# Load order, load sizes and due times in a fused sliding-window attention and squared-ReLU feed-forward kernel

## The chip, the cores and the metric

The kernel runs on one core of one Trainium2 chip. The metric is the device time of one execution in microseconds (us); before the change its median over five runs is 309.8 us (309.5 to 310.71). A core has five engines that run side by side: TensorE (PE) for matrix products and transposes, with its weight loads (PEld), VectorE (DVE), ScalarE (ACT), GpSimd (POOL) and SyncE (SP). In this kernel POOL and SP mostly issue transfers between the chip's memory and the core's own; sixteen DMA engines carry them out.

## The reference

```python
# q, k, v: 8 batches, 8 heads, 576 positions, 64 channels, float32
scores = scale * np.matmul(q, k.transpose(0, 1, 3, 2))      # scale = 1/8
bias = slopes[:, None, None] * (-np.abs(rel))[None]         # rel = query pos - key pos
mask = (rel >= 0) & (rel < 128)
scores = np.where(mask, scores + bias[None], -1e9)
attn = softmax(scores)
x = np.matmul(attn, v)               # then (8*576, 512): heads side by side
h = x @ w_in                         # w_in: 512 x 2048
g = np.maximum(h, 0.0) ** 2
out = g @ w_out                      # w_out: 2048 x 512, out: 4608 x 512 float32
```

A query sees itself and the 127 positions before it, so a block of 128 queries needs the keys of its own block and of the block before.

## The kernel before

Each batch of 576 positions is cut into five blocks, four of 128 and one of 64, so there are 40 blocks, b0 to b39. The 4608 tokens are also cut into nine groups of 512 for the feed-forward part, whose hidden width of 2048 is cut into 16 slices of 128 (the code calls one slice `fc`).

**One block of attention.** POOL loads k, q and v of a block from float32 to bf16 (line 445); SP loads k and q of block 0 alone as float32 (437). k and q are transposed so that channels lie on the partitions: block 0 on TensorE in float32 (497), blocks 1 to 8 on TensorE in bf16 (515), with copies out by DVE or ACT (462, 464), and blocks 9 to 39 by a DMA transpose that SP issues (487). This makes a tile `kqT`. The score products of one or more blocks then run as one uninterrupted run of small matmuls on quarters or halves of the array (`burst`, 570 and 579). ACT takes exp: into tiles `raw` for the blocks that are cut into quarters (612), into `P` for the others (645). DVE multiplies by a mask that holds window and bias (627, 652). TensorE multiplies P by v, with a column of ones that yields the row sum (673). DVE divides (696, 701) and leaves a tile `x`. `x` is turned into `xT` by TensorE for the blocks listed in `X_PE` (719) and by a DMA transpose from SP for the others (711).

**Feed-forward.** `fc_step` (777) multiplies 4 chunks of `w_in` with a stretch of `xT` into a bank of 512 columns: one slice for 512 tokens, two for 256, four for 128. `SPLIT` says into which token ranges groups 0 and 1 are cut; all others are taken whole. ACT applies ReLU (786), DVE squares (793). `t_part` (840) multiplies by `w_out`, sixteen matmuls into one bank for each 128 tokens; ACT copies out (809) and a DMA stores (817), nearly always from SP.

**What sets the order.** All work is first entered in a list of tasks, each with a key. `Plan.order` walks through an assumed time: on each engine it takes the task that can start first and, among equals, the one with the smallest key, and writes the order down. The emitted program keeps this order on every engine; each engine runs its own list in order and stops where an operand is not there. Keys of the loads at the start follow the string `FIRST`, in which `b3` is block 3 (its k, q and v), `i0` the first piece of `w_in` and `o0` the first quarter of `w_out`; `V0` makes v of block 0 a little later. `W_IN` gives the limits of the pieces of `w_in` in slices. Keys of the attention of a block follow from the token at which it is due, less `AHEAD` for that block (or `LEAD`); `EARLY` shifts the first-layer work of group 1. `KQ_PE` and `X_PE` list the blocks that TensorE transposes. Score runs join the halves of several blocks: two halves to a run below block `LONG`, and `UNITS` from it on. `MARGIN` is a time that the planner adds to each landing of a transfer. `SHARE` and `SOON` limit how many banks the feed-forward part may take when a score run is near. At most eight transfers of POOL are under way: the next one waits for the landing of the one eight before.

**Filler.** While the planner expects TensorE to have nothing to do, matmuls on a tile of zeros are put in (`idle`, 880): `WARM` units of 128 columns at the very start, later a share `FILL` of each expected gap up to `UNTIL`. `COLD` is the time up to which the planner counts TensorE's work double.

Of the kernel before, what the change touches and what calls it, by code (L numbers as in the profile page):

```python
# [243 lines left out]
def kernel(  # L244
# [15 lines left out]
    NG = NT // 512  # L260
    NBLK = B * NKB

    FIRST = "b0 b1 b2 b3 i0 i1 o0 b4 i2 b5 i3 o1 b6 b7 o2 b8 o3 b9"
    SPLIT = {0: [(0, 256), (256, 512)], 1: [(0, 192), (192, 320), (320, 512)]}
    EARLY = -60
    AHEAD = {10: -60, 1: 0, 4: 90, 9: 90, 5: -30, 0: -60, 12: 60, 11: 0, 2: 90, 8: 90, 7: 0, 6: 0, 3: -30, 24: 30, 14: 60, 18: 30, 25: 90, 23: 0, 16: 60, 13: 90, 21: 0, 19: -60, 17: 0, 22: 0, 20: 0, 15: 30}
    LEAD = 0

    KQ_PE = [0, 1, 2, 3, 4, 5, 6, 7, 8]
    X_PE = [0, 1, 2, 3, 4, 5, 6, 7, 8, 10, 12]  # L270
    WARM = 20
    FILL, UNTIL = 0.9, 26e3
    COLD = 12000
    QUARTERS = 6
    V0 = 2
    SHARE, SOON = 3, 1000
    MARGIN = 500
    LONG, UNITS = 5, 3
    W_IN = [0, 4, 8, 12, 16]
    PAIR_AFTER, PAIR_KEY = 1, -100  # L280
    BANKS = {"A": 8}
    HOLD, OSB = 12, 14
# [17 lines left out]
    def ring(name, n, shape):  # L300
        return [const.tile(shape, BF16, name=f"{name}_{i}") for i in range(n)]


    size = {"kq": 6, "v": 6, "kqT": 5, "P": 2, "x": 4, "Pq": 2, "raw": 2}
    kq = ring("kq", size["kq"], [128, 2, d_model])
    vt = ring("vt", size["v"], [128, H, D + 1])
    kqT = ring("kqT", size["kqT"], [128, 2 * C, 128])
    Pt = {nm: ring(nm, size[nm], [128, H, 2, 128]) for nm in ("P", "Pq")}
    raw = ring("raw", size["raw"], [128, H, 256])
    xt = ring("x", size["x"], [128, d_model])  # L310

    plan = Plan({"rec": 4, "rt": 3, "g": 2, "osb": OSB, **size}, BANKS, COLD, (SHARE, SOON))
    banks = {tag: [psum.tile([128, 512], FP32, name=f"{tag}_{i}", bufs=1) for i in range(n)] for tag, n in BANKS.items()}
# [84 lines left out]
    def warm():  # L398
        idle(bank(sw), WARM)
    sw = Slot("A")  # L400
    tw = plan.add({"PE": 53.5 * WARM}, -9.1e5, warm, [t_ones], [sw], [sw])
    tw.cols, tw.n = 128 * WARM, -(-WARM // 4)

    def load(key, ns, emit, deps=(), acq=(), cost=13.6):
        return plan.add({"POOL": 900.0}, key, emit, deps, acq, dma=("w", ns, cost))
# [4 lines left out]
    def load_w_in(n, key):  # L410
        lo, hi = 128 * W_IN[n], 128 * W_IN[n + 1]

        def emit():
            nc.gpsimd.dma_start(w_in_sb[:, :, lo:hi], moe_w_in[:, lo:hi].rearrange("(c p) f -> p c f", p=128))  # L414
        t = load(key, {256: 1400.0, 512: 2600.0}[hi - lo] + (700.0 if n == 0 else 0.0), emit, cost=80.0)
        t_win[W_IN[n]:W_IN[n + 1]] = [t] * (W_IN[n + 1] - W_IN[n])

# [32 lines left out]

    for i, what in enumerate(FIRST.split()):
        {"b": load_block, "i": load_w_in, "o": load_w_out}[what[0]](int(what[1:]), -9e5 + i)
# [13 lines left out]
    def where(m):  # L466
        b, kb = divmod(m, NKB)
        return b, kb, blk[kb], (b * S + kb * 128 + blk[kb]) / 4 - 192 - 40 - AHEAD.get(m, LEAD if m not in X_PE else 0), b == 0

    def bank(slot):  # L470
        if slot.tile is None:
            slot.tile = banks[slot.tag][slot.idx]
            if slot.turns:
                slot.tile = slot.tile.bitcast(BF16)
        return slot.tile
# [181 lines left out]
    def mix(m):  # L657
        b, kb, n, due, first = where(m)
        x_by_dma = m not in X_PE
        parts = parts_of[m]  # L660
# [101 lines left out]
    def fc_step(g, unit, key, lo=0, hi=512):  # L762
        if g not in g_slots:
            g_slots[g] = Slot("g")
            g_sq[g] = [[] for _ in range(FCB)]
        sg = g_slots[g]
        w = hi - lo
        per = 512 // w
        slot = Slot("A")
        slot.ffn = True  # L770
        fcs = range(unit * per, min(FCB, (unit + 1) * per))
        cols = len(fcs) * w
        last = None
        for fi, fc in enumerate(fcs):
            for cc in range(C):
                def emit(cc=cc, fc=fc, fi=fi):
                    nc.tensor.matmul(bank(slot)[:, fi * w:(fi + 1) * w], w_in_sb[:, cc, fc * 128:(fc + 1) * 128],  # L777
                                     xT[:, cc, g * 512 + lo:g * 512 + hi], start=cc == 0, stop=cc == C - 1)
                last = plan.add({"PE": mm(w)}, key + (fi * C + cc) * w / 512, emit,
                                [last, t_win[fc]] + tokens(g * 512 + lo, g * 512 + hi),  # L780
                                [slot, sg] if cc == 0 and fi == 0 else [])
        srt = Slot("rt")

        def relu():
            srt.tile = work.tile([128, 512], BF16, tag="rt", bufs=3, name="rt")
            nc.scalar.activation(srt.tile[:, 0:cols], slot.tile[:, 0:cols], AF.Relu, bias=0.0, scale=1.0)  # L786
        tr = plan.add({"ACT": act(cols)}, key, relu, [last], [srt], [slot])

        def square():
            if sg.tile is None:  # L790
                sg.tile = work.tile([128, FCB, 512], BF16, tag="g", bufs=2, name="g")
            r = srt.tile[:, 0:cols].rearrange("p (f w) -> p f w", f=len(fcs))
            nc.vector.tensor_tensor(sg.tile[:, fcs[0]:fcs[-1] + 1, lo:hi], r, r, op=ALU.mult)  # L793
        ts = plan.add({"DVE": dve(cols, 2)}, key, square, [tr], [], [srt])
        for fc in fcs:
            g_sq[g][fc].append((lo, hi, ts))
# [3 lines left out]
    LAST = [(0, 384), (384, 512)]  # L800
    odd = (2 + NBLK - len(KQ_PE) + NBLK - len(X_PE) + NG * 4 + 1) % 8

# [57 lines left out]
    def steps(g):  # L860
        return [(u, lo, hi) for lo, hi in SPLIT.get(g, [(0, 512)]) for u in range(-(-FCB // (512 // (hi - lo))))]

# [4 lines left out]
    for g in range(NG):  # L867
        todo = steps(g + 1) if g + 1 < NG else []
        each = 64 / max(1, len(todo))
        for u in range(16):  # L870
            for x in todo[u * len(todo) // 16:(u + 1) * len(todo) // 16]:
                fc_step(g + 1, x[0], key + (EARLY if g == 0 else 0), *x[1:])
                key += each
# [3 lines left out]
    def idle(tile_, n):  # L877
        for i in range(0, n, 4):
            w = min(4, n - i)
            nc.tensor.matmul(tile_[:, 0:128 * w].rearrange("p (w x) -> p w x", w=w), zero,  # L880
                             zero.unsqueeze(1).to_broadcast([128, w, 128]), start=True, stop=True)

    def filler(slot, n):
        def emit():
            bank(slot)
            idle(banks[slot.tag][slot.idx], n)
        t = Task({"PE": 53.5 * n}, 0, emit, [t_ones], [slot])
        t.eng, t.start, t.end, t.seq, t.cols, t.n = "PE", 0.0, 0.0, 0, 128 * n, -(-n // 4)
        return t

    def fill(tasks):
        at, out = 0.0, []
        for t in tasks:
            if t.eng == "PE":
                slots = [s for s in t.acq if s.tag in BANKS]
                if slots and at and t.start < UNTIL:
                    n = int((t.start - at) * FILL / (107.0 if t.start < COLD else 54.0))
                    if n > 0:
                        out.append(filler(slots[0], n))
                at = t.start + t.engs["PE"] * (2 if t.start < COLD else 1)  # L900
            out.append(t)
        return out

    done = fill(plan.order(MARGIN))
    with tc.manual_schedule():
# [32 lines left out]
```

## Time and profile before

| What | Value |
| --- | --- |
| Median of five runs | 309.8 us |
| The profiled execution | 309.5 us, its span 307.7 us |
| Granted TensorE clock | 1.00 |
| PE busy | 301.0 us, 98% |
| DVE, ACT, POOL busy | 170.8, 170.5, 107.4 us |
| DMA queue of POOL (q0) | 114896 packets, 18.88 MB |
| DMA queue of SP (q1) | 53696 packets, 20.65 MB |
| L840, second layer | 592 matmuls, 146.3 us |
| L777, first layer | 768 matmuls, 145.3 us |
| L880, filler | 30 matmuls |
| L719, x turns on TensorE | 44 matmuls (11 blocks) |

Matmuls overlap, so the duration of one (373 ns on average at L840) is longer than the distance from one start to the next; the timeline's stretches show that distance (20 matmuls of 512 columns in 4.32 us on the chain, 216 ns each). "A <- B" names the tile written and the tiles read; the name after an arrow in brackets is what ended the wait before the instruction. A line number is that of the listing above.

### The profile page before, as it was taken

Reading aid. Unit: us, or ns where it says so; the run is one execution under the profiler, and the core shown is the slowest. Engines: PE = TensorE matmul, PEld = TensorE weight load, DVE = VectorE, ACT = ScalarE, POOL = GpSimd, SP = SyncE. Lnnn points to the kernel's source line nnn. Section 1 sums busy time; section 2 is a strip of 40 time slices with the busy share of each in tenths; the row PEclk is TensorE's granted clock in tenths of the full one; section 3 lists DMA queues with packets and bytes.
Section 4 is the critical chain, followed back from the end, with each engine's and each line's share of the span. In section 5 each row is a group of like instructions: output and inputs, shape, how many; then the busy total and the mean of one; then the engine's idle time right before and its main releaser. Section 6 shows DMA issues by size and latency. Waiting matters only on the chain.

```text
span 307.7 us, 7879 instructions
## 1 busy us (share of the span) xinstructions
PE 301.0 (98%) x3138; PEld 168.0 (55%) x3138; DVE 170.8 (55%) x563; ACT 170.5 (55%) x338; POOL 107.4 (35%) x134
## 2 busy tenths in 40 slices
PE   7799999999999999999999999999999999999996
PEld 3478877785555455455544454455445454444443
DVE  7774767757368865666754674376457552222200
ACT  4965775485157854664664673367366544344411
POOL 8937578545556446055333352110100000000100
PEclk9999999999999999999999999999999999999999
DMA  9999999999999999999999999579911111000022
GB/s 130 151 190 187 175 185 146 143 151 149 127 147 177 134 162 177 118 124 123 156 219 218 164 170 151 134 135 187 208 53 53 52 52 46 34 34 36 34 99 72
DMA packets 168629, 40.04 MB, mean 130 GB/s; under 512 B 159952, under 2 KB 164304, under 8 KB 168592
## 3 DMA queue, kind: packets, MB, share of 16 engines
q0 software_dynamic: 114896, 18.88, 85.3%
q1 hardware_dynamic: 53696, 20.65, 37.7%
q8 instruction: 24, 0.39, 0.5%
q14 instruction: 13, 0.11, 0.1%
HBM read 36.70 MB, written 9.44 MB: 150 GB/s over the span
## 4 chain that ended last, share of the span: by engine, by line
PE 92%; POOL 3%; DMA 3%; issue 0%; DVE 0%; POOLq 0%
PE A L840 41%; PE A L777 40%; PE A L673 5%; DMA w_in_sb<-in_moe_w_in_dram 3%; PE A L570 3%; POOL kq L445 2%; PE A L579 1%; POOL vt L445 1%; PE A L515 1%; PE A L719 1%; POOL w_in_sb L414 0%; POOL dist L326 0%; PE A L880 0%; DVE osb L811 0%; POOLq L326 0%
## 5 line engine op out<-in xcount | busy, mean ns | idle before, releaser
L840 PE MATMUL A<-w_out_sb,g 128*128 128x512 bf16 (+2 forms) x592 | 146.3, 373 | 0.0
L777 PE MATMUL A<-xT,w_in_sb 128*128 128x512 bf16 (+3 forms) x768 | 145.3, 326 | 0.1
L786 ACT ACTIVATE rt<-A 128x512 bf16<-128x512 f32 (+1 forms) x148 | 86.1, 592 | 85.1 <-PE A L777 77.3
L793 DVE TENSOR_TENSOR g<-rt 128x512 bf16<-128x512 bf16 (+1 forms) x148 | 60.9, 415 | 76.2 <-ACT rt L786 75.3
L777 PEld LDWEIGHTS <-w_in_sb 128*128 128x128 bf16 x768 | 68.4, 98 | 50.7 <-DMA w_in_sb<-in_moe_w_in_dram 0.4
L840 PEld LDWEIGHTS <-g 128*128 128x128 bf16 x592 | 54.1, 98 | 55.7 <-issue 0.2
L445 POOL DMA_DIRECT2D vt<-in_v_dram x40 | 33.8, 849 | 82.0 <-PE A L673 77.7
L627 DVE TENSOR_TENSOR Pq<-raw,masks 64x256 bf16<-64x256 bf16 (+1 forms) x168 | 42.9, 285 | 13.2 <-ACT raw L612 10.5
L445 POOL DMA_DIRECT2D kq<-in_k_dram x39 | 33.6, 861 | 24.0 <-DMA kqT<-kq 18.4
L809 ACT ACTIVATE osb<-A 128x512 f32<-128x512 f32 (+1 forms) x36 | 21.5, 597 | 32.2 <-PE A L840 32.1
L612 ACT ACTIVATE raw<-A 128x384 bf16<-128x384 f32 x84 | 35.6, 503 | 6.3 <-PE A L570 6.2
L445 POOL DMA_DIRECT2D kq<-in_q_dram x39 | 33.6, 862 | 4.4 <-DMA w_in_sb<-in_moe_w_in_dram 2.1
L701 DVE TENSOR_TENSOR x<-A,rec 128x256 bf16<-128x256 f32 (+1 forms) x80 | 32.5, 417 | 1.2 <-DVE rec L696 0.2
L817 POOL DMA_DIRECT2D out_dram<-osb x3 | 1.7, 562 | 71.8 <-ACT osb L809 71.8
L645 ACT ACTIVATE P<-A 128x512 bf16<-128x512 f32 (+1 forms) x48 | 23.9, 575 | 1.6 <-PE A L579 1.4
L696 DVE RECIPROCAL rec<-A 128x4 f32<-128x4 f32 (+1 forms) x80 | 13.5, 177 | 19.2 <-PE A L673 18.0
L673 PEld LDWEIGHTS <-Pq 128*128 128x128 bf16 x336 | 15.3, 97 | 8.1
L673 PE MATMUL A<-vt,Pq 128*128 128x65 bf16 x336 | 16.7, 193 | 0.0
L673 PEld LDWEIGHTS <-P 128*128 128x128 bf16 x240 | 10.8, 98 | 5.4 <-DVE P L652 0.8
L652 DVE TENSOR_TENSOR P<-P,pair_masks 128x512 bf16<-128x512 bf16 x28 | 11.6, 421 | 2.9 <-ACT P L645 1.9
L673 PE MATMUL A<-vt,P 128*128 128x65 bf16 x240 | 11.8, 193 | 0.7 <-ACT P L645 0.7
L570 PEld LDWEIGHTS <-kqT 64*64 64x64 bf16 x672 | 8.5, 108 | 5.9 <-issue 5.9
(43 smaller groups left out, 110.3 us busy)
## 6 DMA issues: line engine op xcount, KB each, us to landing
out_dram<-osb SPq DMA_DIRECT2D x32, 256.0 KB, 3.5
vt<-in_v_dram POOLq DMA_DIRECT2D x32, 128.0 KB, 6.3
kq<-in_k_dram POOLq DMA_DIRECT2D x31, 128.0 KB, 7.3
kq<-in_q_dram POOLq DMA_DIRECT2D x31, 128.0 KB, 7.4
w_in_sb<-in_moe_w_in_dram POOLq DMA_DIRECT2D x4, 512.0 KB, 9.1
w_out_sb<-in_moe_w_out_dram POOLq DMA_DIRECT2D x4, 512.0 KB, 10.1
out_dram<-osb POOLq DMA_DIRECT2D x3, 256.0 KB, 2.3
kq<-in_k_dram POOLq DMA_DIRECT2D x8, 64.0 KB, 8.9
```

The costliest lines, as they stand in the source:

```text
L445: nc.gpsimd.dma_start(o, src[b, :, kb * 128:kb * 128 + n, :].rearrange("h s d -> s h d"))
L570: nc.tensor.matmul(slots[m, 2 * j + half].tile[k0:k0 + 64, lo:lo + q1 - q0], kqT[sk_of[mk].idx][rows, c, k0:k0 + 64], kqT[sk_of[m].idx][ro ...
L612: nc.scalar.activation(raw[sr.idx][:, 2 * i:2 * i + 2, 0:192], slot.tile.rearrange("p (c x) -> p c x", c=2)[:, :, 0:192], AF.Exp, bias=0.0 ...
L627: nc.vector.tensor_tensor(o, r, mk, op=ALU.mult)
L645: nc.scalar.activation(Pv(i), view(slot.tile.rearrange("p (c x) -> p c x", c=2)), AF.Exp, bias=0.0, scale=scale)
L673: nc.tensor.matmul(bank(slot_v)[:, hi * (D + 1):(hi + 1) * (D + 1)], Pt[sP.tag][sP.idx][:, place(h)].rearrange("p t q -> p (t q)")[:, at_o ...
L701: nc.vector.tensor_tensor(xt[sx.idx][0:n, hf * 256:(hf + 1) * 256].rearrange("p (h e) -> p h e", h=4), pv[0:n, :, 0:D], srec.tile[0:n, :]. ...
L777: nc.tensor.matmul(bank(slot)[:, fi * w:(fi + 1) * w], w_in_sb[:, cc, fc * 128:(fc + 1) * 128], xT[:, cc, g * 512 + lo:g * 512 + hi], star ...
L786: nc.scalar.activation(srt.tile[:, 0:cols], slot.tile[:, 0:cols], AF.Relu, bias=0.0, scale=1.0)
L793: nc.vector.tensor_tensor(sg.tile[:, fcs[0]:fcs[-1] + 1, lo:hi], r, r, op=ALU.mult)
L809: nc.scalar.activation(so.tile[:, lo:hi], slot.tile[:, lo:hi], AF.Copy)
L840: nc.tensor.matmul(bank(slot)[:, lo:hi], sg.tile[:, fc, t * 128:(t + 1) * 128], w_out_sb[:, fc, lo:hi], start=fc == 0, stop=fc == FCB - 1)
```

## The change

Fourteen settings change, and with them the order that the planner writes. No function changes. The first piece of `w_in` stands ahead of block 0 in the order of loads (block 0's k and q come by SP as before). `w_in` comes in six pieces of 256 columns and one of 512 instead of four of 512. Group 0 is cut into four ranges of 128 tokens instead of two of 256; group 1 into two (192 and 320) instead of three. Block 7's x is turned by DMA. There is a third `raw` tile. Score runs take three units only from block 13 on, instead of block 5. The planner's landing margin is 0, its filler share 0.5, and the due times of 15 blocks differ.

```diff
-    FIRST = "b0 b1 b2 b3 i0 i1 o0 b4 i2 b5 i3 o1 b6 b7 o2 b8 o3 b9"
-    SPLIT = {0: [(0, 256), (256, 512)], 1: [(0, 192), (192, 320), (320, 512)]}
-    EARLY = -60
-    AHEAD = {10: -60, 1: 0, 4: 90, 9: 90, 5: -30, 0: -60, 12: 60, 11: 0, 2: 90, 8: 90, 7: 0, 6: 0, 3: -30, 24: 30, 14: 60, 18: 30, 25: 90, 23: 0, 16: 60, 13: 90, 21: 0, 19: -60, 17: 0, 22: 0, 20: 0, 15: 30}
-    LEAD = 0
+    FIRST = "i0 b0 b1 i1 b2 b3 i2 i3 i4 b4 i5 b5 i6 o0 b6 o1 b7 b8 o2 o3 b9"
+    SPLIT = {0: [(0, 128), (128, 256), (256, 384), (384, 512)], 1: [(0, 192), (192, 512)]}
+    EARLY = -40
+    AHEAD = {10: -60, 1: 30, 4: 90, 9: 90, 5: -30, 0: -60, 12: 30, 11: 30, 2: 60, 8: 60, 7: 0, 6: 0, 3: -60, 24: 60, 14: 30, 18: -60, 25: 90, 23: 0, 16: 60, 13: 30, 21: 60, 19: 30, 17: 0, 22: 90, 20: 60, 15: -30}
+    LEAD = 20
...
-    X_PE = [0, 1, 2, 3, 4, 5, 6, 7, 8, 10, 12]
-    WARM = 20
-    FILL, UNTIL = 0.9, 26e3
-    COLD = 12000
+    X_PE = [0, 1, 2, 3, 4, 5, 6, 8, 10, 12]
+    WARM = 28
+    FILL, UNTIL = 0.5, 26e3
+    COLD = 8200
...
-    SHARE, SOON = 3, 1000
-    MARGIN = 500
-    LONG, UNITS = 5, 3
-    W_IN = [0, 4, 8, 12, 16]
+    SHARE, SOON = 3, 500
+    MARGIN = 0
+    LONG, UNITS = 13, 3
+    W_IN = [0, 2, 4, 6, 8, 10, 12, 16]
...
-    size = {"kq": 6, "v": 6, "kqT": 5, "P": 2, "x": 4, "Pq": 2, "raw": 2}
+    size = {"kq": 6, "v": 6, "kqT": 5, "P": 2, "x": 4, "Pq": 2, "raw": 3}
```

In the built programs TensorE's list has 3138 matmuls before and 3167 after; filler goes from 13,056 to 10,496 columns, L777 from 768 to 832 matmuls, L719 from 44 to 40; the score runs become 26 instead of 23. POOL's list has three more loads of w_in and issues four of the stores instead of three.

## The prediction

> **What bounds the kernel now.** I read the page's busy shares first, then the chain that ended last, then TensorE's timeline of the first 45 us, then busy time by stage.
>
> ```profile
> PE 301.0 (98%) x3138; PEld 168.0 (55%) x3138; DVE 170.8 (55%) x563; ACT 170.5 (55%) x338; POOL 107.4 (35%) x134
> PE   7799999999999999999999999999999999999996
> DMA  9999999999999999999999999579911111000022
> ```
>
> TensorE is busy 98% of the span and every other engine about half of it, so the time moves only by TensorE's own work and by its waits. The chain says where the one long wait is:
>
> ```profile
> 10.73 0.66 POOL w_in_sb L414
> 11.38 9.62 DMA w_in_sb<-in_moe_w_in_dram
> 21.68 1.42 PE A L777 x13
> ```
>
> The end follows back to the w_in loads, which POOL issues only after 12 loads of q, k and v. The timeline of TensorE shows what that costs:
>
> ```profile
> 13.04 0.40 PE L515 MATMUL A<-ident,kq 128*128 128x128 bf16 x4 [0.26 <-DMA kq<-in_k_dram]
> 13.86 0.40 PE L515 MATMUL A<-ident,kq 128*128 128x128 bf16 x4 [0.42 <-DMA kq<-in_q_dram]
> ...
> 18.53 0.22 PE L880 MATMUL A<-zero 128*128 128x128 bf16 x1
> 18.58 1.91 PE L777 MATMUL A<-xT,w_in_sb 128*128 128x256 bf16 x16
> 20.33 0.41 PE L673 MATMUL A<-vt,P 128*128 128x65 bf16 x8
> 20.57 0.38 PE L880 MATMUL A<-zero 128*128 128x512 bf16 x1
> 21.05 0.39 PE L777 MATMUL A<-xT,w_in_sb 128*128 128x256 bf16 x2
> ...
> 23.27 0.49 PE L880 MATMUL A<-zero 128*128 128x512 bf16 x2
> 23.77 0.81 PE L840 MATMUL A<-w_out_sb,g 128*128 128x512 bf16 x3
> ```
>
> The first useful feed-forward matmul starts at 18.58; in the trace the first w_in load landed at 18.46 and the second at 21.00. L880 rows are filler, so a busy TensorE is not a useful one here. By stage:
>
> ```profile
> 10.00:15.00 5.00, 3.63 (x62) 2.46 (x60) 4.25 (x16) 4.61 (x10) 5.00 (x8) 1.00 1.91 152
> 20.00:25.00 5.00, 4.89 (x54) 3.64 (x51) 2.82 (x9) 2.62 (x5) 1.86 (x3) 1.00 1.56 192
> ...
> 26.00:40.00 14.00, 14.00 (x172) 12.04 (x171) 8.88 (x26) 10.19 (x20) 9.57 (x12) 1.00 1.86 180
> 60.00:80.00 20.00, 20.00 (x289) 13.45 (x288) 12.32 (x45) 10.81 (x23) 9.70 (x13) 1.00 2.13 150
> ```
>
> Columns: stretch, its length, then busy time of PE, PEld, DVE, ACT, POOL, the clock, DMA share and GB/s. From 26 us on TensorE waits for nothing at all. What can be gained lies ahead of about 25 us; anything later can only be lost.
>
> **The loads, moved.** POOL now issues w_in piece 0 (256 of 2048 columns) first, then k and q of block 1, v0, piece 1, v1, and blocks 2 and 3; pieces 2 to 4; block 4; piece 5; block 5; piece 6 (512 columns); then the first w_out. Prices: the first POOL load landed 4.4 us after its issue; block loads then land one by one, 0.82 us apart (13.04 to 13.86 above); POOL waits for w loads 2.6 us apart, so a piece of half the bytes is 1.3. Bounds for the piece: 0.42 (512 packets at the pace of block loads, 1024 in 0.85) and 1.7 (its 512 KB read at the block loads' 256 KB per 0.85); I take 1.3, by bytes from its own kind. Estimated landings: piece 0 at 6.2, k1 7.0, q1 7.9, v0 8.8, piece 1 10.1, v1 11.0, k2 11.9, q2 12.7, q3 15.3, v3 16.2, pieces 2, 3, 4 at 17.5, 18.8, 20.1, piece 5 22.8, block 5 25.3, piece 6 27.9, first w_out 30.5 (before 23.7, but nothing needs it: its first matmul now stands later in the order). Blocks 0 to 3 with 1024 columns of w_in are there at 18.8 instead of 21.00; k2 and q2 come 3 us later than before (8.9 and 9.7). Three more issues at L414 are 3 x 0.83 = 2.5 us of POOL, ahead of every later load; they cost nothing, since POOL stood waiting for landings 2.09 + 2.06 + 1.46 us between 16 and 24 us. Without that cover, 2.5 us on every load.
>
> [...] I go by the trace: 7 pieces 6 x 1.3 + 2.6 = 10.4, as 4 x 2.6 before.
>
> **TensorE up to 18.5 us.** Following the new order with rows of the trace: ScalarE's masks end near 7.6 (7.78 before; the iota stands behind a 0.83 issue instead of 1.05); kqT of block 0 8.15; scores of block 0 to 8.4; turn of block 1 to 8.85; two exps, then kqT of block 1 to 9.7; its scores to 10.35; P times V of block 0 10.8; the turn of block 2 waits for q2, 12.95; P times V of block 1 and the x turn of block 0, 13.75; scores of block 2 14.5; **first FFN matmuls at 14.5** instead of 18.58; they are now 128 columns wide, so one block's x is enough. The turn of block 3 ends at 15.55, P times V of half of block 2 at 16.55, x turn of block 1 at 16.8; eight FFN matmuls wait for piece 2 and end at 17.95; scores of block 3 end at 18.5.
>
> At that point the new order has done all that the old one had at 18.58, except half of P times V of block 2 (8 x 0.029 = 0.23) and one x turn (4 x 0.056 = 0.22), and has 24 FFN matmuls more (24 x 0.056 = 1.34). Lead: 1.34 - 0.45 + 0.08 = **0.97 us**. After 18.58 the old order still spends 0.48 (20.57 to 21.05) and 0.50 (23.27 to 23.77) on filler and waiting; the new one has no filler behind its sixteenth FFN matmul but two at about 16 us, counted above, and by the landings above each piece is there before its matmuls: **0.98 us**. Together 1.95. Bounds: q2 and piece 2 may land 0.6 earlier, or 1.5 later, in which case these 1.5 are lost entirely.
>
> **Fixed work on TensorE.** One x turn less: 4 x 0.056 = -0.22. Groups 0 and 1 in other widths, start to start 56, 82.5 and 109 ns for 128, 192 and 256 columns and 136 by that line for 320: 256 x 56 + 64 x 82.5 + 64 x 136 = 28.3 against 128 x 109 + 128 x 82.5 + 64 x 56 = 28.1: +0.2. Score runs: between FFN matmuls a run of 48 (three units) costs 0.74 from the end of the one before to the next, of which 0.2 is the change over; mixed runs 0.81 and 0.87. With units of two until block 13, 22 runs instead of 20 stand behind 26 us: 15.7 against 15.3: +0.4. Together **+0.4**.
>
> **The x turn of block 7** goes to SP: one more DMA transpose, with its own issue (about 1.2 us of SP) and some 8.5 us to landing, as the old trace's first such turn. It stands behind the kqT turn of block 9, so about 48 to 57; kqT of block 10 is queued behind it, 1.2 us later, some 3 us before its scores. The matmuls that read x of block 7 stand 14 us behind its P times V, so it costs nothing; were those gone, 8 us.
>
> **The rest.** The third raw tile lets exp of a third block start before the masks of the first are done; L612's largest idle time was for TensorE (6.2 us), so nothing. Four more relu and square pairs are 2.4 us of engines that are half idle. The due times only reorder. **The planner's margin** of 500 ns on every landing becomes 0: what is placed just behind its landing can now stop TensorE. The old trace has such places: the scores at 84.30 read a kqT that landed at 83.62. Bounds: 0, and 3.2 us (that transpose's 12.3 us to landing less the usual 9.1). I take 0.3, near 0, because the loads are 2 us earlier as well as TensorE.
>
> **Sum**: -1.95 + 0.4 + 0.3 = -1.25. The profiled execution took 309.5 (span 307.7 and 1.8 around it), so 308.2 or 308.3; it lies 0.3 under the median of 309.8, so the median becomes **308.5**.
>
> **Rivals.**
> (a) *The early start starves.* FFN begins at 14.5 but the pieces land late, the lead becomes waits ahead of 30 us: 309.8 + 0.4 = 310.2; for it: TensorE runs ahead on 128 columns and one piece serves only 0.9 us per block; against: 10.8 us of FFN work is unlocked at 22.8. If three quarters are lost, 309.8 - 0.5 + 0.4 = 309.7, no change.
> (b) *Slower, through the margin:* kqT of a block near 80 us lands later than planned and TensorE stands, since its order is fixed. A landing 3.2 late costs 3.2 + 0.4 - 1.95 = +1.65, 311.4. It decides from 1.55 us on. For it: 0.68 of slack, 150 GB/s and a DMA row of nines there; against: not one such wait before.
> (c) *More gain:* q2 and piece 2 land 0.6 earlier and nothing stalls: -1.95 - 0.6 + 0.4 = -2.15, 307.6.
> [...]
>
> **Chances.** Forecast (faster by 0.6 to 2.0) 0.50; (c) 0.12; (a) with no clear change 0.16; (b) 0.18; (d) 0.04. About 0.2%, 0.6 us, is what this measurement can tell from no change. So faster 0.62, same 0.16, slower 0.22. The range leaves out the best part of (c) and the worst of (b): 306.9 to 311.3; the forecast's own is 307.8 to 309.2.
>
> **What would show it.** Right: first L777 near 14.5; no L880 behind 17 us; scores of block 3 end near 18.5; from 26 us PE busy as long as the stretch; L719 x40. Wrong: idle time of PEld at L777 put down to w_in, at L570 or L579 to kqT, or at L515 to kq behind 20 us; the time between first L777 and 30 us full of waits; filler at 427 ns behind 6 us.

## The result, and the profile after

The kernel after takes 309.51 us (median of 39 executions, 308.8 to 310.34), the kernel before, timed beside it, 310.26 us (76 executions). The medians are 0.75 us apart, where 1.3 us were forecast. The ratio of the times is 0.9971, with a 95% interval of 0.996 to 0.9983 (the quotient of the two medians, 0.9976, lies in it): faster by 0.2 to 0.3%. The median of before is not the same on every occasion (310.26 here, 310.43 to 310.66 beside the kernels below), so each kernel's ratio to the before timed beside it is given with its median.

The two profiled executions do not show this gain. Before took 309.5 us with a span of 307.7, after 309.56 with a span of 307.8. The first execution of before that was profiled was one of its quick ones: 0.8 us under the median that the many later executions gave. So the difference of the medians cannot be read from these two profiles alone.

The page of after (busy time of each engine, then the span in 40 slices of 7.7 us, then the group of first-layer matmuls):

```profile
PE 299.7 (97%) x3167; PEld 165.9 (54%) x3167; DVE 167.5 (54%) x566; ACT 171.4 (56%) x342; POOL 110.4 (36%) x138
PE   6699999999999999999999999999999999999996
DMA  9999999999999999999999999999422120010022
L777 PE MATMUL A<-xT,w_in_sb 128*128 128x512 bf16 (+3 forms) x832 | 146.4, 314 | 0.3 <-DMA w_in_sb<-in_moe_w_in_dram 0.3
```

TensorE is busy for 1.3 us less than before in the same span: 2560 columns of filler are gone, but the first two slices read 6 and 6 where before had 7 and 7. TensorE's timeline of after shows where those slices are empty (start, length, the instructions, and in brackets the idle time before them and what ended it):

```profile
8.17 0.40 PE L579 MATMUL A<-kqT 64*128 64x128 bf16 x8 [1.39 <-ACT kqT L464]
10.37 0.23 PE L579 MATMUL A<-kqT,kqT 64*128 64x128 bf16 x2 [0.60 <-ACT kqT L464]
12.48 0.42 PE L673 MATMUL A<-vt,P 128*128 128x65 bf16 x8 [1.17 <-DMA vt<-in_v_dram]
12.74 0.86 PE L880 MATMUL A<-zero 128*128 128x512 bf16 x4
14.02 0.40 PE L515 MATMUL A<-ident,kq 128*128 128x128 bf16 x4 [0.19 <-DMA kq<-in_q_dram]
...
16.11 0.68 PE L777 MATMUL A<-xT,w_in_sb 128*128 128x128 bf16 x9
17.46 0.54 PE L880 MATMUL A<-zero 128*128 128x512 bf16 x2
18.74 0.62 PE L777 MATMUL A<-xT,w_in_sb 128*128 128x128 bf16 x8 [0.27 <-DMA w_in_sb<-in_moe_w_in_dram]
...
19.85 0.42 PE L673 MATMUL A<-vt,P 128*128 128x65 bf16 x8
20.10 1.33 PE L777 MATMUL A<-xT,w_in_sb 128*128 128x128 bf16 x21
```

The first feed-forward matmul starts at 16.11, 2.5 us sooner than before, but not at 14.5. P times V of block 0 stands 1.17 us for its v, and the scores of block 3 end just ahead of 19.85, not at 18.5. The last filler is the group at 17.46, and from 20.10 on there is no wait of note. By stretch (length, then busy time of PE, PEld, DVE, ACT, POOL, the clock, DMA share, GB/s):

```profile
10.00:15.00 5.00, 3.27 (x52) 2.23 (x51) 2.85 (x11) 3.40 (x9) 5.00 (x7) 1.00 2.39 156
20.00:25.00 5.00, 5.00 (x103) 4.98 (x100) 4.21 (x16) 3.75 (x8) 3.74 (x6) 1.00 2.14 169
60.00:80.00 20.00, 20.00 (x241) 12.52 (x240) 13.22 (x51) 12.56 (x30) 7.69 (x9) 1.00 2.32 156
```

Between 20 and 25 us TensorE is full (4.89 before, part of it filler), and between 60 and 80 it is full as before, with no planner's margin any more.

Two figures are used below. One is the start of the first L777. The other is how far the two feed-forward layers have come: the time at which 16,384 columns of L777 and L840 have been started, counted from the trace. It is 27.7 us in the first profile of before and 27.4 in that of after.

### The profile page after: what moved, and what is told of

It is laid out like the page before. It is cut to its first block, busy times and chain, and to the rows that moved or that the text cites. A ratio compares the mean times of both kernels' runs of the same rounds, so it can differ in the third digit from the quotient of the medians.

```text
span 307.8 us, 7940 instructions
## 1 busy us (share of the span) xinstructions
PE 299.7 (97%) x3167; PEld 165.9 (54%) x3167; DVE 167.5 (54%) x566; ACT 171.4 (56%) x342; POOL 110.4 (36%) x138
## 4 chain that ended last, share of the span: by engine, by line
PE 93%; POOL 3%; DMA 2%; issue 1%; DVE 0%; POOLq 0%
PE A L777 41%; PE A L840 41%; PE A L673 5%; PE A L570 3%; DMA w_in_sb<-in_moe_w_in_dram 2%; PE A L579 2%; POOL kq L445 1%; POOL vt L445 1%; PE A L515 1%; PE A L719 1%; POOL w_in_sb L414 1%; POOL dist L326 0%; DVE osb L811 0%; POOLq L326 0%; POOLq L922 0%
## 5 line engine op out<-in xcount | busy, mean ns | idle before, releaser
L777 PE MATMUL A<-xT,w_in_sb 128*128 128x512 bf16 (+3 forms) x832 | 146.4, 314 | 0.3 <-DMA w_in_sb<-in_moe_w_in_dram 0.3
L840 PE MATMUL A<-w_out_sb,g 128*128 128x512 bf16 (+2 forms) x592 | 143.5, 373 | 0.0
L786 ACT ACTIVATE rt<-A 128x512 bf16<-128x512 f32 (+2 forms) x152 | 86.0, 582 | 78.7 <-PE A L777 72.8
L793 DVE TENSOR_TENSOR g<-rt 128x512 bf16<-128x512 bf16 (+2 forms) x152 | 60.9, 405 | 84.1 <-ACT rt L786 83.4
L777 PEld LDWEIGHTS <-w_in_sb 128*128 128x128 bf16 x832 | 67.4, 98 | 48.7 <-DMA w_in_sb<-in_moe_w_in_dram 0.4
L840 PEld LDWEIGHTS <-g 128*128 128x128 bf16 x592 | 55.0, 98 | 58.4
L627 DVE TENSOR_TENSOR Pq<-raw,masks 128x256 bf16<-128x256 bf16 (+1 forms) x168 | 43.3, 285 | 13.5 <-ACT raw L612 11.0
L652 DVE TENSOR_TENSOR P<-P,pair_masks 128x512 bf16<-128x512 bf16 x28 | 11.7, 418 | 6.3 <-ACT P L645 5.4
L673 PE MATMUL A<-vt,P 128*128 128x65 bf16 x240 | 12.5, 193 | 1.3 <-DMA vt<-in_v_dram 1.2
```

What stands on the lines that cost most here:

```text
L627: nc.vector.tensor_tensor(o, r, mk, op=ALU.mult)
L673: nc.tensor.matmul(bank(slot_v)[:, hi * (D + 1):(hi + 1) * (D + 1)], Pt[sP.tag][sP.idx][:, place(h)].rearrange("p t q -> p (t q)")[:, at_o ...
L840: nc.tensor.matmul(bank(slot)[:, lo:hi], sg.tile[:, fc, t * 128:(t + 1) * 128], w_out_sb[:, fc, lo:hi], start=fc == 0, stop=fc == FCB - 1)
```

## The experiments

### One setting: v of block 0 back in its place

The trace of after has v of block 0 landing at 12.44, behind piece 1 of `w_in` (11.43). `V0` adds 2 to that load's key; with `i0` at the head of the list block 0 has key 1, so its v sorts behind `i1`.

```diff
-    V0 = 2
+    V0 = 1
```

> The changed kernel with V0 = 1: v of block 0 is loaded ahead of piece 1 of w_in. Theory A (the early loads eat the gain: v of block 0 lands at 12.44 and TensorE stands 1.17 us for it): P times V of block 0 starts near 11.4 instead of 12.48, the first feed-forward matmul stays gated by q of block 2 (13.97) and comes at most 0.5 earlier than 16.11, time 0.1 to 0.6 us below the changed kernel (about 309.1). Theory B (fixed TensorE work in the split and the score runs eats it): no difference from the changed kernel, 309.5.

Measured: 308.92 us (308.54 to 309.89), ratio to before 0.9943 (0.992 to 0.9966), span 307.0. On TensorE's timeline P times V of block 0 starts 1.7 us sooner and the feed-forward part 0.6 sooner:

```profile
10.82 0.30 PE L673 MATMUL A<-vt,P 128*128 128x65 bf16 x4
...
15.49 0.73 PE L777 MATMUL A<-xT,w_in_sb 128*128 128x128 bf16 x10
```

The 16,384 columns are reached at 26.6 us instead of 27.4. The late v of block 0 is therefore what took back part of the lead: the start is 0.6 us earlier, the columns 0.8, the span 0.8 (307.0 against 307.8). Between the medians lie 0.6 us, at the upper end of theory A, but not all of that has to be the load: none of these 14 executions has a mean clock near 0.994 and 11 of after's 40 have it (see the last experiment). At full clock alone the distance is 0.35 us (308.92 against 309.27), and the two ratios' intervals touch.

### The cuts alone, and the cuts with the loads

The first kernel is before with only the column cuts of after; the second also has its load order and load sizes.

```diff
-    SPLIT = {0: [(0, 256), (256, 512)], 1: [(0, 192), (192, 320), (320, 512)]}
+    SPLIT = {0: [(0, 128), (128, 256), (256, 384), (384, 512)], 1: [(0, 192), (192, 512)]}
```

```diff
-    FIRST = "b0 b1 b2 b3 i0 i1 o0 b4 i2 b5 i3 o1 b6 b7 o2 b8 o3 b9"
+    FIRST = "i0 b0 b1 i1 b2 b3 i2 i3 i4 b4 i5 b5 i6 o0 b6 o1 b7 b8 o2 o3 b9"
...
-    W_IN = [0, 4, 8, 12, 16]
+    W_IN = [0, 2, 4, 6, 8, 10, 12, 16]
```

> The kernel before with the new SPLIT alone (group 0 in four ranges of 128, group 1 in 192 and 320); loads as before. Theory A: feed-forward still waits for the first w_in load at 18.5, so there is no lead; only the 0.2 us of extra matmul time less some filler after 18.58: within 0.4 us of the kernel before. Theory B: 0.2 to 0.6 us slower than before.

> The kernel before with the new FIRST, W_IN and SPLIT alone; due times, margin, score runs, x turn, filler and raw tiles as before. Theory A: these three make the whole gain; without the third of score runs (+0.4) and with the x turn (+0.2) it is as fast as the changed kernel or up to 0.4 us faster: ratio to before 0.996 to 0.998. Theory B: no gain, ratio 1.000 or above.

Measured: the cuts alone 311.44 us, ratio 1.0026 (1.0006 to 1.0047), first L777 at 18.27 and 16,384 columns at 27.3; that is 1.0 us over the median of before timed beside it, more than either expectation had. Cuts and loads 310.79 us, ratio 1.0009 (0.999 to 1.0029), first L777 at 16.07 and 16,384 columns at 27.1. Both are at that point as early as after. So the loads bring the early start, and the early start alone brings no time. The waits of TensorE behind 26 us say where it went. Each row has the waiting line, what it waited for, total us, times, longest. With the cuts alone:

```profile
PE A L840 <- DMA w_out_sb<-in_moe_w_out_dram: 0.6, 1, 0.6
PE A L777 <- DVE xT L462: 0.5, 1, 0.5
PE A L777 <- DVE x L701: 0.2, 1, 0.2
PE A L673 <- DVE Pq L627: 0.2, 1, 0.2
```

With the cuts and the loads:

```profile
PE A L673 <- DVE Pq L627: 0.8, 1, 0.8
PE A L777 <- DVE x L701: 0.2, 1, 0.2
```

The place of the second is TensorE's timeline at 88.90, where P times V of a block cut into quarters waits for DVE's masks:

```profile
88.90 0.42 PE L673 MATMUL A<-vt,Pq 128*128 128x65 bf16 x8 [0.84 <-DVE Pq L627]
```

TensorE came to this place earlier, the chain of scores, exponentials and masks did not, and the order on TensorE is fixed: about 1 us was handed back some 60 us later. The view of waits of after has no row at all behind 26 us. The expectation that loads and cuts make the whole gain fell.

### The loads without the cuts

This is after with the column cuts of before.

```diff
-    SPLIT = {0: [(0, 128), (128, 256), (256, 384), (384, 512)], 1: [(0, 192), (192, 512)]}
+    SPLIT = {0: [(0, 256), (256, 512)], 1: [(0, 192), (192, 320), (320, 512)]}
```

> The kernel after with the column cuts of before (groups of 256 + 256 and 192 + 128 + 192). Theory: the cuts matter only through the first groups, since a 256-column group needs two weight pieces' rows no earlier than a 128-column one; the fixed work falls by about 0.2 us (128 matmuls fewer of 128 columns) and the first FFN matmul stands within 0.7 us of that of after (16.1 us): ratio 0.995 to 0.998. Rival: the narrow groups are what the early FFN work is cut to; without them filler or waits ahead of 26 us grow by 1 us or more and the ratio is 1.000 to 1.003.

Measured: 311.24 us, ratio 1.0024 (1.0004 to 1.0045): 1.7 us over after, so the rival holds and the expectation of a small gain was wrong. TensorE's timeline has the reason:

```profile
18.93 0.23 PE L579 MATMUL A<-kqT,kqT 64*128 64x128 bf16 x2 [0.41 <-DVE kqT L462]
...
19.73 1.36 PE L777 MATMUL A<-xT,w_in_sb 128*128 128x256 bf16 x11
```

A matmul of 256 columns needs the x of two blocks, so it can't start before the x turn of block 1, at 17.87, with the scores of block 3 behind it. Filler stands at 16.00, 16.69 and 18.13 where after has feed-forward work. The 16,384 columns are reached at 29.1 us. In this execution, which took 312.35 us and so 1.1 over its kernel's median, the view of waits behind 26 us also has

```profile
PE A L579 <- DMA kqT<-kq: 1.3, 1, 1.3
```

at 64 us: a score run stood for a transposing DMA. So the gain of after needs the narrow cuts. They are not enough for it: the cuts alone (311.44) and the cuts with the loads (310.79) are no faster than before either.

### The settings that only order or guard

Three kernels, each after with one thing put back: the margin; the due times `AHEAD`, `LEAD` and `EARLY` of before; two `raw` tiles.

```diff
-    MARGIN = 0
+    MARGIN = 500
```

```diff
-    EARLY = -40
+    EARLY = -60
...
-    LEAD = 20
+    LEAD = 0
```

(and the table `AHEAD` of before)

```diff
-    size = {"kq": 6, "v": 6, "kqT": 5, "P": 2, "x": 4, "Pq": 2, "raw": 3}
+    size = {"kq": 6, "v": 6, "kqT": 5, "P": 2, "x": 4, "Pq": 2, "raw": 2}
```

> The changed kernel with the planner's margin back at 500. Forecast's allowance of 0.3 us for stalls behind 25 us: 0.0 to 0.3 us faster. As the trace of the changed kernel shows no wait of TensorE behind 20 us beyond the change over of score runs, theory A expects no difference above 0.3 us from the changed kernel in either direction. If the margin hides late landings in executions other than the profiled one, 0.5 us or more faster.

> The changed kernel with AHEAD, LEAD and EARLY of the kernel before. The load and split run had the same early start (first feed-forward matmul 16.07) but waits of TensorE of 1.0 and 0.4 us at 88 to 91 us. Theory D: the new due times are what keeps the lead, by placing the attention of blocks 13 to 16 earlier against the feed-forward work: without them waits of 1 to 2 us behind 60 us, time 310.2 to 311.2. Rival (due times only reorder, as the forecast had it): 309.2 to 309.8, no wait behind 26 us.

> The kernel after with two raw tiles, as before. Theory R (the third raw tile keeps the lead near 88 us): a TensorE wait of 0.8 to 1.4 us for Pq or x between 60 and 92 us comes back, span 308.5 to 309.2, ratio 1.000 to 1.002. Theory N (raw does nothing but reorder): no wait above 0.3 us behind 26 us, span 307.3 to 308.0, ratio 0.995 to 0.998.

| Kernel | Median, us | Ratio to before | TensorE's wait behind 26 us |
| --- | --- | --- | --- |
| after | 309.51 | 0.9971 (0.996 to 0.9983) | none |
| margin back | 309.24 | 0.9964 (0.9947 to 0.9981) | none |
| due times back | 309.1 | 0.995 (0.9932 to 0.9968) | none |
| two raw tiles | 309.44 | 0.9969 (0.9954 to 0.9984) | none over 0.2 each |

In this table "none over 0.2 each" stands for six gaps of 0.2 us with nothing that ended them, in a trace that lacks 39 of its matmul records; each is as long as one matmul, and need not be a wait. The intervals overlap with that of after in all three, that of the due times by very little, and there on the faster side. None of these settings carries the gain, and none is what keeps TensorE from waiting near 88 us. The theory that the due times do so fell with the second row, the theory of the third raw tile with the third.

### All of it but the filler, the x turn, the margin and the raw tile

This is before with the loads, the cuts, the due times and `LONG` of after. It keeps before's `WARM`, `FILL`, `COLD`, `SOON`, `MARGIN`, `X_PE` and two raw tiles.

```diff
-    LONG, UNITS = 5, 3
+    LONG, UNITS = 13, 3
```

(with `FIRST`, `W_IN`, `SPLIT`, `AHEAD`, `LEAD` and `EARLY` of after)

> The kernel before with the change's load order, widths, column cuts, due times (AHEAD, EARLY, LEAD) and LONG of 13, but with before's WARM, FILL, COLD, SOON, its margin of 500, its x turns on TensorE and two raw tiles. Theory L (LONG and the due times keep the early lead from being handed back near 88 us): first FFN matmul between 15.5 and 16.5 us, less than 0.5 us of TensorE waits behind 26 us, profiled span 306.9 to 308.0, median ratio 0.995 to 0.998. Theory R (the third raw tile or the moved x turn keeps it): the wait for Pq or x between 86 and 92 us is still there with 0.8 to 1.4 us, span about 308.8, ratio 1.000 to 1.002 as with loads and cuts alone.

Measured: 310.92 us, ratio 1.0012 (0.9995 to 1.0028). No wait for Pq or x near 88 us is in its profile, as theory L has it, and yet the time is that of theory R: neither theory had the place of the loss. The traces have it. This kernel reaches the 16,384 columns at 28.3 us and the one with two raw tiles at 27.5, and the spans are 308.9 and 308.0: nearly the whole difference is there ahead of 28 us, though the first L777 (16.48) is only 0.5 later. TensorE's timeline shows the largest piece of it:

```profile
18.84 0.65 PE L880 MATMUL A<-zero 128*128 128x512 bf16 x3
19.32 0.50 PE L777 MATMUL A<-xT,w_in_sb 128*128 128x128 bf16 x6
20.19 0.23 PE L777 MATMUL A<-xT,w_in_sb 128*128 128x128 bf16 x1 [0.37 <-DMA w_in_sb<-in_moe_w_in_dram]
...
20.98 0.23 PE L579 MATMUL A<-kqT,kqT 64*128 64x128 bf16 x2
```

From 18.84 to 20.19 there is 0.48 us of filler and 0.37 of waiting for piece 3 (landed at 20.14). The scores of block 3 stand behind that in the order and start at 20.98, though their `kqT` was copied out by 19.26; after has them at 19.29.

What is left between this kernel and the one with two raw tiles (309.44) is 1.5 us and the settings `WARM`, `FILL`, `COLD`, `SOON` and the x turn, if the margin is worth as little here as it is in after. The filler may be part of it: behind 5 us this kernel's list has 8960 columns of filler and that one's 6912, and the 2048 more are 4 matmuls of 0.216 us, 0.86 at most. It need not be: the filler at 18.84 ends before piece 3 lands, so without it TensorE would have reached the same wait sooner. The x turn on TensorE is 4 x 0.056 = 0.22. `COLD` and `SOON` also change the order that the planner writes. Which of these settings makes the 1.5 us was not separated, since no run puts the filler alone back.

### Two more orders of the loads

Both have `V0 = 1`. In one, piece 1 comes behind block 2; in the other, piece 0 comes behind block 1's k and q.

```diff
-    FIRST = "i0 b0 b1 i1 b2 b3 i2 i3 i4 b4 i5 b5 i6 o0 b6 o1 b7 b8 o2 o3 b9"
+    FIRST = "i0 b0 b1 b2 i1 b3 i2 i3 i4 b4 i5 b5 i6 o0 b6 o1 b7 b8 o2 o3 b9"
```

```diff
-    FIRST = "i0 b0 b1 i1 b2 b3 i2 i3 i4 b4 i5 b5 i6 o0 b6 o1 b7 b8 o2 o3 b9"
+    FIRST = "b0 b1 i0 b2 i1 b3 i2 i3 i4 b4 i5 b5 i6 o0 b6 o1 b7 b8 o2 o3 b9"
```

> The changed kernel with V0 = 1 and piece 1 of w_in moved behind block 2: k and q of block 2 and v of blocks 0 to 2 land about 1.3 us earlier, piece 1 near 15. Theory A: scores of block 2 start near 14.3 instead of 15.55, first feed-forward matmul near 15.2; 0.3 to 1.0 us below the changed kernel, like the run with v ahead or better: 308.5 to 309.2. If the gate is piece 2 (18.7, the same bytes ahead of it): the same as v ahead, 308.9.

> The kernel after with V0 = 1 and the first weight piece queued behind the k and q of block 1 and not ahead of them. If the first two k and q loads gate the start (they would land some 1.3 us earlier, the scores of block 1 start by 9 us, the weight piece lands by about 8.5 us, ahead of its need at 15.5): 16384 FFN columns by 26.0 to 26.4 us, ratio 0.990 to 0.993. Rival (what gates is the v and P of the first block and ScalarE's exponentials, as with piece 1 late): 16384 columns by 26.5 to 27.0 as in the kernel with V0 = 1 alone, ratio 0.993 to 0.996.

Piece 1 later: 308.78 us, ratio 0.9949 (0.9929 to 0.997). The first L777 moves from 15.49 to 16.86, not to the 15.2 expected, but 16,384 columns are reached at 26.6 us as with piece 1 early: what TensorE loses at the one end it gains in attention work done sooner (the scores of block 2 start at 13.44 instead of 14.94). Piece 0 later: 309.8 us, ratio 0.9979 (0.996 to 0.9998), with 16,384 columns at 26.7 us. The columns are as the rival had them; the time is slower than both of its sides, and the expectation that the first k and q gate the start is wrong. Its timeline shows what came in the place of the wait removed:

```profile
9.75 0.29 PE L673 MATMUL A<-vt,P 128*128 128x65 bf16 x4
...
12.04 0.40 PE L515 MATMUL A<-ident,kq 128*128 128x128 bf16 x4 [1.09 <-DMA kq<-in_k_dram]
12.94 0.40 PE L515 MATMUL A<-ident,kq 128*128 128x128 bf16 x4 [0.50 <-DMA kq<-in_q_dram]
```

P times V of block 0 starts 1.1 us sooner than with `V0 = 1` alone, but k and q of block 2, behind piece 0 (landed at 11.15), land at 12.00 and 12.89, only 0.5 us sooner than there, and TensorE now waits for them. In after, the loads that POOL issued in the first 12 us landed one after the other, 0.7 to 1.4 us apart; here, with one moved ahead, the wait moved to another.

### Before, profiled twice more

Why is the first profile of before 0.8 us under its median? The kernel before was run and profiled twice more.

> The kernel before, unchanged, profiled again. Its times spread over 308.5 to 316 us where those of the changed kernel lie within 308.8 to 310.3, and its first profiled execution (309.5) was 0.8 below its median. Theory C: the median is higher because in many executions a landing is late and TensorE waits behind 25 us; an execution of 310 us or more then shows waits of TensorE on a DMA or on an engine behind one, summing to the excess over 307.7 of span. Rival: the excess lies ahead of 25 us (the first loads) or outside the span; then no wait of TensorE stands behind 25 us.

> The kernel before, unchanged, a third look. As for the second: theory C expects an execution above 310 us to carry its excess as waits of TensorE behind 25 us; the rival expects it ahead of 25 us or outside the span.

The second profile has a span of 310.1 and its first L777 at 21.47 instead of 18.58. The busy time of PE by stretch, with the granted clock behind it:

```profile
8.25:11.65 3.40, 1.75 (x32) 0.96 2.21 141
11.65:18.10 6.45, 6.17 (x60) 0.50 1.56 184
```

The timeline of that execution has the wait ahead of it, and filler at 430 ns to the 512 columns:

```profile
11.93 0.60 PE L673 MATMUL A<-vt,P 128*128 128x65 bf16 x8 [1.52 <-ACT P L645]
12.34 1.36 PE L880 MATMUL A<-zero 128*128 128x512 bf16 x3
```

From 11.65 to 18.10 TensorE had half its clock. No wait of TensorE stands behind 26 us, and the 16,384 columns come at 30.0 us, 2.4 later than in the first profile, as much as the span is longer: the rival was right here, and theory C wrong. The third profile has a full clock and a span of 309.2, 1.4 over the first. Its first L777 is 0.75 late (19.33), of which 0.2 is left at the 16,384 columns (27.9), and one wait stands behind 26 us, at 89 us:

```profile
PE A L777 <- DMA xT<-x: 1.1, 1, 1.1
```

So here theory C was right for the most part. In the first profile the same matmul started at 88.81, 0.135 us after its xT had landed, which is how soon it also started in the third at the end of its wait: it had no slack. So before loses time at places where it has next to no slack, in some executions and not in others, and its first profile was one without such a loss. Two more profiles are few: they show two places, and not how often each is met.

The half clock is not the difference between the two kernels. In 17 of 73 executions of before (those timed beside the last kernels) the mean clock is about 0.994, as much as one stretch of 3.4 us at half clock makes of 308 (the profile of the kernel with all but the filler has one such, from 8.3 to 11.7, and a mean clock of 0.994), and the median of these is 311.13 against 310.39 for the others; in 11 of 40 of after, 309.95 against 309.27. At full clock alone after is 1.1 us ahead, in so far as executions of two occasions may be set side by side.

## Why the prediction was right, and where not

**The bound and the direction: right.** From 20 us on the profile of after has no filler and TensorE is full. The gain is 0.75 us between medians, inside the range of 0.6 to 2.0 and short of 1.25; the time itself, 309.51, lies above the 307.8 to 309.2 that went with it, since before was at 310.26 and not at 309.8. That only the first 25 us could give time holds for the one profile that the forecast had. The third profile of before has a wait of 1.1 us at 89 us.

**The lead at 18.5 us: this step failed.** It was put at 0.97 us, with the first L777 at 14.5 and the scores of block 3 ending at 18.5. The trace has 16.11 and nearly 19.85, 1.35 us later, so the lead at that point, with the same work done as forecast (24 feed-forward matmuls among it), is 0.97 - 1.35 = -0.38. Two terms were wrong, each worth about half: with `V0 = 1` the scores of block 3 end just ahead of 19.09.

- *The order of the two v loads.* The list of landings had v of block 0 ahead of piece 1, at 8.8. By its key it stands behind piece 1 (v of block 1 took its place), and it landed at 12.44. P times V of block 0, put at 10.8, started at 12.48. Putting `V0` to 1 moves it to 10.82: the row of the forecast was right for an order that this change does not have.
- *The price of the loads.* Piece 0 landed at 7.05, not 6.2, since its DMA took 5.8 us from issue to landing, not the 4.4 of before's first load. Pieces 1 and 2 landed 1.27 and 1.17 behind the load ahead of them, near the 1.3 taken. Pieces 2, 3 and 4 landed at 18.70, 20.51 and 22.12, 1.8 and 1.6 apart, at the upper bound of 1.7; piece 6 at 29.38 instead of 27.9. Leaving the two v loads that changed places aside, everything behind piece 0 was 0.9 to 2.2 us late.

The loads overlap, as the trace of before said: there the first seven loads of POOL took 4.2 to 5.1 us each from issue to landing and landed 0.7 to 1.6 us apart. With three more loads of w_in in after, it was complete at 29.38, against 32.56 before.

**The filler behind 18.58: right.** The 0.98 us of filler and waiting that before has there is gone. That 0.98 less 0.38 of lost lead, and 0.4 of fixed work, make -0.2; the profiled spans differ by +0.1, so 0.3 us of that pair has no row. The last filler of after starts at 17.68, a little behind the 17 that was named.

**Fixed work: right.** L719 has 40 matmuls. The score runs behind 26 us take 13.95 us in 22 runs against 13.44 in 20, from the first score matmul of a run to the matmul behind the run: +0.5 for the 0.4 forecast.

**The margin: harmless.** 0.3 was allowed for stalls. The profile of after shows none, and 500 ns put back change nothing that can be measured.

**The due times "only reorder": right** as far as a run shows it (309.1 with those of before, so no loss), and so was the third raw tile at nothing.

**What was not in the sum.** The forecast took before's time as its profile had it, with a median 0.3 above. Over many executions the median is 0.8 above; two more profiles show losses that the first did not have, one ahead of 20 us and one at 89. The times of after lie within 1.5 us of each other and those of before, in the same comparison, over 8 us. At the tenth percentile before is 0.4 us behind after (309.44 against 309.03), at the ninetieth 2.05 us (312.11 against 310.06). A good part of the gain is that after loses less in its worse executions. The forecast's -1.25 came from a different account, of which -0.2 is left with the measured lead. That 0.75 lies in its range is in good part luck.

**The rivals.** (a) is nearest to what the profiled pair shows: a lead taken back ahead of 20 us; but it named w_in as the late load, and TensorE stood for that 0.27 us only. (b) did not happen in after. Its mechanism is real: cuts and loads alone stood 0.8 us for Pq near 88 us, and after with the old cuts stood 1.3 us for a kqT at 64. (c) is nearest to the kernel with `V0 = 1`, though for another reason than the one it gave. (d), 0.04 in the chances, is a halved clock. The one profile that the forecast had does not show how often that comes; the timed executions do: a mean clock near 0.994 stands in 17 of 73 executions of before and 11 of 40 of after, whose medians lie 0.74 and 0.68 us over those of the others. The 427 ns that the forecast would have taken as its sign is the distance of the first filler matmuls of before, from 1.4 to 3.5 us; behind 5.5 us filler matmuls that follow one another stand 0.216 us apart in both first profiles.

**What stays open.** Profiles of kernels with `LONG` of 13 show no wait over 0.3 us behind 26 us, except for the one with the old cuts; those with `LONG` of 5 show none or up to 1.5 us in all. `LONG` alone was not put back, since the planner finds no order for after with 5, so it isn't shown that it is the cause. Nor is it shown which of `WARM`, `FILL`, `COLD`, `SOON` and the x turn makes the 1.5 us between two of the kernels. Each profile is one execution, and such waits come and go. Nor is it known why the execution times of the kernel with piece 0 late spread more (308.74 to 311.86) than those of after.

## What to carry to other kernels

Write down the order of the loads as the keys give it, load by load, before estimating a landing: one swapped load (0.35 to 0.6 us) was worth more here than the due times of fifteen blocks, which no run shows to be worth anything. The load moved to the head of the queue delayed those behind it: k and q of block 1 landed at 7.95 and 8.79 us, against 5.71 and 7.13 before. It paid only together with work small enough to use it at once (the narrow cuts, and even then not with all the other settings of before). Where a gain of one microsecond is in question, profile the kernel before more than once: its waits at places with next to no slack came and went (1.1 us at 89 us in one of three profiles), and the profiled execution may be the one without them.

## What the runs showed of the hardware

- **The granted clock was halved while TensorE was partly busy.** In the kernel with all but the filler it was 0.50 from 8.3 to 11.7 us, in the second profile of before from 11.3 to 18.2. The first two lines are of that kernel, the next two of that profile, the last of after, which kept its clock:

```profile
4.95:8.35 3.40, 1.43 (x10) 1.00 2.10 163
8.35:11.70 3.35, 3.06 (x23) 0.50 2.07 170
8.25:11.65 3.40, 1.75 (x32) 0.96 2.21 141
11.65:18.10 6.45, 6.17 (x60) 0.50 1.56 184
9.80:13.20 3.40, 1.66 (x28) 1.00 2.35 157
```

  Of the 3.40 us that end within 0.3 us of the loss of the clock TensorE was busy for 1.43 and 1.75, with no single wait over 2.0 us (1.97 ahead of 7.16 and 1.52 ahead of 11.93). Of the 3.40 of after it was busy for 1.66, and no loss stands there. What decides it is not shown by these profiles, and the busy time of TensorE is modelled in part.
- **Loads of POOL overlapped deeply.** In after a load issued in the first 12.2 us took 5.2 to 6.6 us from issue to landing, and yet they landed 0.7 to 1.4 us apart. The seven pieces of w_in took 5.8 to 8.5 us each, 49.1 in all, and landed within 22.3 us (7.05 to 29.38). So the time from issue to landing was not what one more load cost here.
- **Neither bytes nor packets alone gave the price of a piece.** In POOL's queue of after a packet of 128 B took 32 ns on one of the sixteen engines, one of 512 B 60 ns and one of 1024 B 98 ns (medians). By packets a piece of 256 columns is 512 x 60 / 16 = 1.9 us and a block load of 1024 packets 1024 x 32 / 16 = 2.0, nearly the same; but most block loads landed 0.7 to 1.0 us behind the load ahead of them, and pieces 1 to 4 1.2 to 1.8.
